# Batch 0 and batch 1 loaded and staged differently at the start of a pooled-attention and MLP kernel

## The chip, the core and the metric

The kernel runs on one core of a Trainium2 chip. A core has a matrix engine (TensorE, PE in the profile, with its weight loads as PEld), VectorE (DVE), ScalarE (ACT), GpSimd (POOL) and SyncE (SP), and 16 DMA engines that serve the queues of SP, ACT and POOL. In the traces q1 is SP's queue, q10 ScalarE's and q0 GpSimd's, whose transfers also convert fp32 to bf16. The metric is the device time of one execution in microseconds. Four executions of the kernel before took 300.72 to 301.33, median 301.1.

## The reference

q, k and v have 8 batches, 8 heads, 576 tokens and 64 elements a head. k and v are averaged over 8 neighbouring tokens to 72 rows; each batch then does softmax attention. The result, 4608 tokens of 512, goes through a two-layer MLP whose activation is h - tanh(h).

```python
k_p = k.reshape(B, H, Sp, pool, D).mean(axis=3)
v_p = v.reshape(B, H, Sp, pool, D).mean(axis=3)
scores = scale * np.matmul(q, k_p.transpose(0, 1, 3, 2))
attn = softmax(scores)
x = np.matmul(attn, v_p).transpose(0, 2, 1, 3).reshape(B * S, H * D)
h = x @ w_in
out = (h - np.tanh(h)) @ w_out
```

## The kernel before

Attention goes batch by batch, the MLP in 9 groups of 512 tokens. A group has a hidden stage (`mlp_h`: 16 tiles of 4 matmuls, tanh on ScalarE, the difference `gT` on VectorE) and an output stage (`mlp_o`: 4 token blocks of 16 matmuls, in 16 units u of 4 matmuls). The attention of batch g+1 stands between the units of group g's output stage. The order on every engine is the order in which the code is written (`manual_schedule`).

Two heads share 144 pooled rows of k (or v), laid on partitions: the first 128 rows of each of four head pairs form the main tiles 0 to 3, the remaining 16 of each pair form tile 4, the leftovers (`NM`). `pool_k` adds the eight tokens in three steps and writes each row twice (`kd`), TensorE turns it (`turn_tile`), and `kb_main` and `kb_left` place it in `KB`. In batch 0 v is pooled by TensorE instead (`v_pe_pool`, accumulating 8 matmuls against `ident`, or against `spread` for the leftovers); in the others `pool_v` does it with adds. `av_half` multiplies the exponentials `E` with `VB`, divides by the sum that an extra column carries, and writes `x_sb`; `x_pe_transpose` turns that into `xT`, from which `mlp_h` reads.

q has 512 tokens in four interleaved columns (R = 4) and a tail of 64 tokens (`QT`, `load_q_tail`), which come as separate loads, are cast to bf16 (`q_cast`, or `q_turn` for batch 0) and turned by TensorE for batches 0 and 1 (`q_pe_transpose`, `q_pe_tail`), by DMA for the others.

At the start SP loads k of batch 0, ScalarE's queue loads q and the leftovers, and GpSimd's queue loads v of batch 0 (L576), the four quarters of w1 (L503) and the first two of w2 (L510). k of batch 1 waits for the second quarter of w1 (L592, `after`), then come q and v of batch 1 on SP. ScalarE also issues q's tail of batch 0 (L640), v's leftovers of batch 1 (L659, four DMAs) and q's tail of batch 1 (L660). While the data come, `warm_pe` puts matmuls on zeros into TensorE's gaps, 29 in all.

Batch 0's attention (L631 to L690) goes through eight `av_half` and eight `x_pe_transpose` of two feature blocks each; five hidden tiles of group 0 are begun early with two of their four matmuls. Batch 0's last 64 tokens, which belong to group 1, are done in group 0's hidden stage: the tail's turn after tile 7, its scores after 9, its attention after 11, its turn into xT after 13. GpSimd pools k of batch 1 at L707, with the last two quarters of w2 issued between its first and second step. In group 0's output stage batch 1 is done: q cast at u=0, k turned at u=2, q turned at u=3 to 5, v pooled at u=4 (VectorE), scores at u=4 to 8, attention of its five blocks from u=9, each turned two units later.

In the built program a DMA of SP or ScalarE carries one of eight semaphores in turn, so each waits for the DMA eight places before it to land. PSUM has eight banks: three for hidden tiles, two for outputs, three for attention (`ps_a`); within group 0's output stage attention has only the last three (`ps_b1`).

```python
for u in range(16):
    qd, tb = u // 4, u % 4
    mlp_o(0, tb, qd * 4, qd * 4 + 4, gts, o_pools[tb])
```

Of the kernel before, what the change touches and what calls it, by code (L numbers as in the profile page):

```python
# [8 lines left out]
FP32 = mybir.dt.float32  # L9
# [10 lines left out]
R = 4  # L20
QA = 128 * R
QT = S - QA
T = B * S
# [14 lines left out]
def kernel(  # L38
# [19 lines left out]
    ps_h = ctx.enter_context(tc.tile_pool(name="ps_h", bufs=3, space=PSUM))  # L58
    ps_o = ctx.enter_context(tc.tile_pool(name="ps_o", bufs=2, space=PSUM))
    ps_a = ctx.enter_context(tc.tile_pool(name="ps_a", bufs=3, space=PSUM))  # L60
# [9 lines left out]

    w1b = const.tile([128, NFB, DFF], BF16, name="w1b")
# [3 lines left out]
    spread = const.tile([128, 128], BF16, name="spread")  # L75
    mask = const.tile([128, 3 * NM, 1], FP32, name="mask")
# [3 lines left out]
    q_bf = const.tile([128, R + 1, H, D], BF16, name="q_bf")  # L80
    warm = const.tile([128, 1], FP32, name="warm")
# [22 lines left out]
    def load_left(src, dst, b, eng=nc.sync):  # L104
        return [
            eng.dma_start(out=dst[32 * t : 32 * t + LO, NM, :], in_=src[b, 128:PR, t, :])
            for t in range(NM)
        ]
# [5 lines left out]

    def load_k(b):
        return [
            load_main(k_pairs, k_raw[b % 2], b, 0, NM),
            load_dense(k_pairs, k_raw[b % 2], b),
        ]

    def load_v(b):
        return [load_main(v_pairs, v_raw[b % 2], b, 0, NM)] + load_left(
            v_pairs, v_raw[b % 2], b
        )

    def load_q_tail(b, t, eng):
        eng.dma_start(
            out=t[:QT, :, R, :], in_=q[b, :, QA:S, :].rearrange("h p d -> p h d")
        )

    def load_q(b, tail=True):
        if b not in q_raws:
            q_raws[b] = raw.tile([128, H, R + 1, D], FP32, name="q_raw", tag="q_raw")
        t = q_raws[b]
        nc.sync.dma_start(
            out=t[:, :, 0:R, :], in_=q[b, :, 0:QA, :].rearrange("h (p j) d -> p h j d", j=R)
        )
        if tail:
            load_q_tail(b, t, nc.sync)
# [4 lines left out]
    def q_cast(b, eng=nc.gpsimd.tensor_copy, parts=1):  # L144
        t = q_raws.pop(b)
        n = H // parts
        for h in range(0, H, n):
            eng(  # L148
                out=q_bf[:, 0:R, h : h + n, :].rearrange("p j h d -> p h j d"),
                in_=t[:, h : h + n, 0:R, :],  # L150
            )
        eng(out=q_bf[:QT, R, :, :], in_=t[:QT, :, R, :])

    def q_dma_transpose(b):
        qT = work.tile([128, NHP, S], BF16, name="qT", tag="qT")
        for j in range(R + 1):
            rows = 128 if j < R else QT
            nc.sync.dma_start_transpose(
                out=qT[:, :, j * 128 : j * 128 + rows],
                in_=q_bf[:rows, j, :, :].rearrange("p h d -> p (h d)"),  # L160
            )
        qTs[b] = qT

    def q_pe_transpose(b, hps, eng=None):
        if b not in qTs:
            qTs[b] = work.tile([128, NHP, S], BF16, name="qT", tag="qT")
        qT = qTs[b]
        for hp in hps:
            ps = ps_any([128, QA], FP32, "qT_ps")
            for j in range(R):  # L170
                nc.tensor.matmul(  # L171
                    ps[:, j * 128 : (j + 1) * 128],
                    lhsT=q_bf[:, j, 2 * hp : 2 * hp + 2, :].rearrange("p h d -> p (h d)"),
                    rhs=ident[:, :],
                    start=True,
                    stop=True,
                )
            evac(qT[:, hp, 0:QA], ps[:, :], eng)

    def q_pe_tail(b):  # L180
# [9 lines left out]
        evac(qTs[b][:, :, QA:S], ps[:, :, :])  # L190
# [23 lines left out]
    def pool_v(b, eng):  # L214
# [10 lines left out]
        v_main(VB[b % 2], r[:, :, 0:1, :], eng, 0, NM)  # L225
        v_left(VB[b % 2], r[:, NM, 0:1, :], eng)

    def v_main(vb, vs, eng, t0, t1):
# [3 lines left out]
            in0=vs[:, t0:t1, :, :].to_broadcast([128, n, 2, D]),  # L232
# [4 lines left out]
        )  # L237

# [27 lines left out]

    def k_transpose(b, alloc, engs=(nc.vector.tensor_copy, nc.scalar.copy)):
# [5 lines left out]
        ps = alloc([128, 128], FP32, "kT_ps")  # L273
        turn_tile(ps[:, :], kd, NM)
# [18 lines left out]
    def score_mms(b, t, dst, c0, c1, pairs=range(NM)):  # L293
        for m in pairs if t == NM else (t,):
# [11 lines left out]
    def scores(b, t):  # L306
        if t == 0:
            E_tiles[b] = work.tile([128, NT, S], BF16, name="E", tag="E")
        E = E_tiles[b]
        hs = S // 2  # L310
        pss = []
        for half in range(2):
            ps = ps_a.tile([128, hs], FP32, name="s_ps", tag="ps_a")
            score_mms(b, t, ps[:, :], half * hs, (half + 1) * hs)
            pss.append(ps)
        for half, ps in enumerate(pss):
            nc.scalar.activation(  # L317
                out=E[:, t, half * hs : (half + 1) * hs], in_=ps[:, :], func=ACT.Exp, scale=SCALE
            )
# [377 lines left out]
    for i in range(5, NHID):  # L697
        mlp_h(0, i, gts)
        if i == 7:
            q_pe_tail(0)  # L700
# [104 lines left out]
```

The softmax here doesn't subtract the row's maximum and nothing guards it: scores larger than these inputs give would overflow.

## Time and profile before

| what | value |
|---|---|
| median of 4 runs | 301.1 us (300.72 to 301.33) |
| the profiled execution | 300.72 us, its span 299.0 us |
| TensorE busy | 291.5 us, 98% of the span |
| VectorE, ScalarE, GpSimd busy | 159.2, 149.4, 115.2 us |
| MLP matmuls, hidden and output | 126.9 and 134.4 us busy |
| granted TensorE clock | 1.00 throughout |
| DMA, first 60 us | 15.53 MB, mean 259 GB/s |

A span is the time from the first to the last instruction of the profiled execution. Busy times of TensorE are taken instruction by instruction, and matmuls overlap: a 128x512 matmul is given with 0.38 us, while one starts every 0.216 us in an unbroken row. So the time that work takes on TensorE is read from the distance of starts, not from the busy time of one. A "<-" in brackets behind a line names what the engine had waited for, and for how long.

The loads of the start land as follows (issue, time to landing, in us): v of batch 0 3.67 + 8.5; w1's quarters 5.1 + 10.3, 5.85 + 12.8, 6.6 + 15.4, 7.3 + 19.0; w2's first two 8.04 + 23.2 and 11.24 + 24.4, the others 32.98 + 8.7 and 33.7 + 9.6; k of batch 1 18.66 + 10.7, its q 19.87 + 16.6, its v 29.40 + 11.2.

### The profile page before, as it was taken

To read this page: it belongs to the slowest core of one execution; us is meant where nothing else is said; L and a number is where in the kernel's file an instruction comes from. 1 tells how busy PE (TensorE), PEld (TensorE's weight loads), DVE (VectorE), ACT (ScalarE), POOL (GpSimd) and SP (SyncE) were. 2 spreads that over 40 slices of the span, in tenths; PEclk is the share of its full clock that TensorE was granted. 3 is DMA by queue.
4 is the path that set the end of the run, shared out by engine and by line. 5 is a ranking of instruction groups with operands and counts; after the bars stand their busy time and mean duration, and the time that the engine had idled before them with its cause. 6 is when DMAs were issued, how large, how long until landed. Compare 5 with 4: busy or idle time off the path is not lost.

```text
span 299.0 us, 4694 instructions
## 1 busy us (share of the span) xinstructions
PE 291.5 (98%) x1671; PEld 142.4 (48%) x1671; DVE 159.2 (53%) x343; ACT 149.4 (50%) x283; POOL 115.2 (39%) x110
## 2 busy tenths in 40 slices
PE   7989999999999999999999999999999999999994
PEld 3444455544544454445544554455445544444443
DVE  5658665673547444753476247716680758108600
ACT  4647683666146623654265516650665166126511
POOL 8500905870495109924961079408930000000000
PEclk9999999999999999999999999999999999999999
DMA  7999999849854997798648974796421430111032
GB/s 258 221 210 280 312 223 315 259 100 331 217 114 101 280 296 128 120 322 217 108 87 242 309 156 88 261 293 148 96 59 35 91 97 0 37 70 36 2 70 70
DMA packets 66183, 49.79 MB, mean 167 GB/s; under 512 B 39920, under 2 KB 52976, under 8 KB 66160
## 3 DMA queue, kind: packets, MB, share of 16 engines
q1 hardware_dynamic: 58832, 42.94, 55.1%
q0 software_dynamic: 4752, 4.72, 9.4%
q10 hardware_dynamic: 2576, 1.84, 2.2%
q8 instruction: 13, 0.21, 0.3%
q14 instruction: 10, 0.08, 0.1%
HBM read 36.70 MB, written 9.44 MB: 154 GB/s over the span
## 4 chain that ended last, share of the span: by engine, by line
PE 85%; DMA 9%; POOL 4%; issue 0%; SPq 0%; ACT 0%; DVE 0%; POOLq 0%
PE o_ps L456 40%; PE hT_ps L428 37%; DMA w1b<-in_moe_w_in_dram 4%; PE x_ps L346 4%; DMA k_raw<-in_k_dram 4%; PE s_ps L298 3%; POOL k_raw L198 1%; DMA out_dram<-o_sb 1%; POOL k_raw L203 1%; POOL kd L206 1%; POOL w2b L510 0%; PE xT_ps L390 0%; POOL v_raw L576 0%; PE qT_ps L171 0%; POOL w1b L503 0%
## 5 line engine op out<-in xcount | busy, mean ns | idle before, releaser
L456 PE MATMUL o_ps<-w2b,gT 128*128 128x512 bf16 x560 | 134.4, 380 | 0.0
L441 DVE TENSOR_TENSOR gT<-hT_ps,t_sb 128x512 bf16<-128x512 f32 x144 | 98.9, 691 | 57.7 <-ACT t_sb L439 57.6
L428 PE MATMUL hT_ps<-xT,w1b 128*128 128x512 bf16 x576 | 126.9, 379 | 0.3 <-ACT xT L397 0.3
L439 ACT ACTIVATE t_sb<-hT_ps 128x512 f32<-128x512 f32 x144 | 85.6, 597 | 38.3 <-PE hT_ps L428 37.5
L428 PEld LDWEIGHTS <-w1b 128*128 128x128 bf16 x576 | 55.9, 98 | 66.5 <-issue 0.4
L456 PEld LDWEIGHTS <-gT 128*128 128x128 bf16 x560 | 52.5, 98 | 52.1 <-issue 1.4
L465 ACT COPY o_sb<-o_ps 128x512 f32<-128x512 f32 x33 | 19.3, 585 | 75.2 <-PE o_ps L456 75.2
L359 DVE RECIPROCAL rden<-x_ps 128x4 f32<-128x4 f32 x80 | 14.2, 177 | 52.8 <-PE x_ps L346 52.3
L360 DVE TENSOR_TENSOR x_sb<-x_ps,rden 128x256 bf16<-128x256 f32 x80 | 34.0, 425 | 3.6 <-DMA xT<-x_sb 0.7
L148 POOL CAST q_bf<-q_raw 128x2048 bf16<-128x2048 f32 x6 | 11.3, 1888 | 59.8 <-DMA out_dram<-o_sb 36.1
L198 POOL TENSOR_TENSOR k_raw<-k_raw 128x1280 f32<-128x1280 f32 x7 | 20.2, 2887 | 27.1 <-DMA k_raw<-in_k_dram 27.1
L317 ACT ACTIVATE E<-s_ps 128x288 bf16<-128x288 f32 x60 | 21.4, 410 | 13.2 <-PE s_ps L298 13.0
L346 PE MATMUL x_ps<-VB,E 128*128 128x130 bf16 x240 | 20.8, 221 | 0.7 <-ACT xT L397 0.6
L346 PEld LDWEIGHTS <-E 128*128 128x128 bf16 x240 | 16.9, 98 | 9.2 <-issue 0.8
L216 POOL TENSOR_TENSOR v_raw<-v_raw 128x1280 f32<-128x1280 f32 x6 | 17.4, 2898 | 0.0
L298 PE MATMUL s_ps<-qT,KB 128*128 128x288 bf16 (+5 forms) x128 | 17.0, 290 | 0.1
L298 PEld LDWEIGHTS <-KB 128*128 128x128 bf16 (+1 forms) x128 | 7.0, 96 | 10.1 <-issue 3.4
L527 PE MATMUL warm_ps<-xT 128*128 128x512 bf16 x29 | 10.1, 461 | 1.3 <-DVE xT L539 1.3
L206 POOL TENSOR_TENSOR kd<-k_raw 128x640 bf16<-128x640 f32 x7 | 10.8, 1538 | 0.6
L203 POOL TENSOR_TENSOR k_raw<-k_raw 128x640 f32<-128x640 f32 x7 | 10.8, 1539 | 0.5
L397 ACT CAST xT<-xT_ps 128x256 bf16<-128x256 f32 (+1 forms) x14 | 5.8, 436 | 8.9 <-PE xT_ps L390 8.7
L219 POOL TENSOR_TENSOR v_raw<-v_raw 128x640 f32<-128x640 f32 x6 | 9.3, 1545 | 0.5
(73 smaller groups left out, 100.6 us busy)
## 6 DMA issues: line engine op xcount, KB each, us to landing
k_raw<-in_k_dram SPq DMA_DIRECT2D x7, 1024.0 KB, 6.0
q_raw<-in_q_dram SPq DMA_DIRECT2D x7, 1024.0 KB, 9.7
v_raw<-in_v_dram SPq DMA_DIRECT2D x7, 1024.0 KB, 9.0
out_dram<-o_sb SPq DMA_DIRECT2D x38, 128.0 KB, 2.4
out_dram<-o_sb SPq DMA_DIRECT2D x16, 256.0 KB, 3.0
w1b<-in_moe_w_in_dram POOLq DMA_DIRECT2D x4, 512.0 KB, 14.1
w2b<-in_moe_w_out_dram POOLq DMA_DIRECT2D x4, 512.0 KB, 16.9
k_raw<-in_k_dram SPq DMA_DIRECT2D x7, 128.0 KB, 5.9
```

What stands on the lines that cost most here:

```text
L198: first = eng.tensor_tensor(out=r[:, :, 0:4, :], in0=r[:, :, 0:4, :], in1=r[:, :, 4:8, :], op=ALU.add)
L216: eng.tensor_tensor(out=r[:, :, 0:4, :], in0=r[:, :, 0:4, :], in1=r[:, :, 4:8, :], op=ALU.add)
L298: nc.tensor.matmul(dst[p : p + w], lhsT=KB[b % 2][:, o : o + w], rhs=qTs[b][:, m, c0:c1], start=True, stop=True,)
L317: nc.scalar.activation(out=E[:, t, half * hs : (half + 1) * hs], in_=ps[:, :], func=ACT.Exp, scale=SCALE)
L346: nc.tensor.matmul(ps[:, 2 * n : 2 * n + 2, :].rearrange("p h d -> p (h d)") if n < 2 else ps.rearrange("p (a s) d -> p a s d", s=2)[:, :, ...
L359: nc.vector.reciprocal(out=rden[:, :, :], in_=ps[:, :, D:D1])
L360: nc.vector.tensor_tensor(out=x_sb[:, half, :, :], in0=ps[:, :, 0:D], in1=rden[:, :, :].to_broadcast([128, 4, D]), op=ALU.mult,)
L428: nc.tensor.matmul(h_tiles[i][:, :], lhsT=w1b[:, fb, i * 128 : (i + 1) * 128], rhs=xT[:, fb, tok0 : tok0 + TG], start=(fb == 0), stop=(fb ...
L439: nc.scalar.activation(out=t_sb[:, :], in_=h_ps[:, :], func=ACT.Tanh)
L441: nc.vector.tensor_sub(out=gT[:, :], in0=h_ps[:, :], in1=t_sb[:, :])
L456: nc.tensor.matmul(o_ps[:, :], lhsT=gts[i][:, tb * 128 : (tb + 1) * 128], rhs=w2b[:, i, :], start=(i == 0), stop=(i == NHID - 1),)
L465: (nc.vector.tensor_copy if g == 0 and tb % 2 else nc.scalar.copy)(out=o_sb[:, :], in_=o_ps[:, :])
```

## The change

- The leftovers of batches 0 and 1 come as half rows (4 of the 8 tokens) over all 128 partitions, as `load_halves`, in place of whole rows over 64 partitions or, for v of batch 1, of four DMAs. The two halves of a row are joined by the matmul that turns them: k's leftovers are added in two VectorE (batch 0) or GpSimd (batch 1) steps into an fp32 tile `k_left` and turned against the fp32 `twos`; v's of batch 0 are pooled with four matmuls against a `spread` that has two ones a column, and v's of batch 1 are added into the fp32 `vl` and spread by one fp32 matmul.
- The loads of batch 1 on SP are in the order k, halves of k, halves of v, q's tail of batch 0, q in two DMAs, v. ScalarE issues no DMA after its first five. q of batch 1 has nine neighbouring tokens a partition (`q_nine`, 2304-byte rows), so that it has no separate tail; its output rows are stored in the matching order (`NINE`, `out_segments`).
- w2's second quarter, and those after it, wait for k of batch 1; the third and fourth are issued between GpSimd's steps on k.
- v of batch 0 is pooled in two halves. The attention of batch 0 is divided in pairs of blocks, two PSUM banks with one reciprocal and one multiply (`av_pair`), and turned in pairs (`x0_turn`). PSUM is one tile with banks named by hand. 24 warm-up matmuls are left of 29.
- Batch 0's last 64 tokens move from group 0's hidden stage to its output stage (u=0, 1, 8, 11). Batch 1's steps there stand one unit later, each unit is cut in two for the last turn at u=15, and batch 1's last block moves to group 1's hidden stage.
- Later loads of k (from batch 3 on) and v (from batch 6 on) are cut in two DMAs.

```diff
+    def load_halves(src, dst, b, eng=nc.sync):
+        return eng.dma_start(out=dst[:, NM, 0:HALF], in_=src[b, 2 * 128 : 2 * PR, :, :])
+    q_nine = q.rearrange("b (s a h) (p j) d -> b s p a h (j d)", s=2, a=2, j=NJ)
...
+    def pool_k_left(b, eng):
+        r = k_raw[b][:, NM, 0:HALF].rearrange("p (j d) -> p j d", d=D)
+        eng.tensor_tensor(out=r[:, 0:2, :], in0=r[:, 0:2, :], in1=r[:, 2:4, :], op=ALU.add)
+        eng.tensor_tensor(
+            out=k_left[b][:, :, :],
+            in0=r[:, 0:1, :].to_broadcast([128, 2, D]),
+            in1=r[:, 1:2, :].to_broadcast([128, 2, D]),
+            op=ALU.add,
+        )
+    def pool_v1(eng):
...
+        eng.tensor_tensor(out=vl[:, :], in0=r[:, NM, 0, :], in1=r[:, NM, 1, :], op=ALU.add)
...
+    def v1_left():
+        ps = ps_any([128, 1, D], FP32, "v_ps")
+        nc.tensor.matmul(ps[:, 0, :], lhsT=spread32[:, :], rhs=vl[:, :], start=True, stop=True)
+        v_left(VB[1], ps, nc.vector)
+    def turn_left(dst, b):
+        nc.tensor.matmul(
+            dst, lhsT=k_left[b].rearrange("p a d -> p (a d)"), rhs=twos[:, :], start=True, stop=True
+        )
...
-    nc.vector.memset(k_raw[0][:, NM, :], 0.0)
-    nc.vector.memset(v_raw[1][:, NM, :], 0.0)
...
+    nc.gpsimd.memset(q_bf[64:128, R, :, :], 0.0)
+    nc.gpsimd.memset(spread[:, :], 0.0)
     nc.gpsimd.dma_start(out=v_bf[:, 0:NM, :], in_=v_pairs[0, 0:128, :, :])
-    nc.gpsimd.memset(spread[:, :], 0.0)
+    nc.gpsimd.tensor_tensor(out=twos.rearrange("p (x t) -> p x t", t=NM), ...)
...
-    load_w2(1)
-    after(load_k(1), w1_dmas[1])
-    load_q(1, False)
+    k1 = load_main(k_pairs, k_raw[1], 1, 0, NM)
+    after([k1], w1_dmas[1])
+    load_halves(k_halves, k_raw[1], 1)
+    load_halves(v_halves, v_raw[1], 1)
+    load_q_tail(0)
+    load_q_nine(1, 0, nc.sync)
+    load_q_nine(1, 1, nc.sync)
     load_main(v_pairs, v_raw[1], 1, 0, NM)
+    load_w2(1)
+    after(w2_dmas[1:], k1)
+    pool_k(1, nc.gpsimd, 0, NM)
+    load_w2(2)
+    pool_k_left(1, nc.gpsimd)
+    load_w2(3)
...
+    def av_pair(p, half, b0):
+        ps = PS[:, b0 : b0 + 2, 0 : 4 * D1].rearrange("p k (h d) -> p k h d", d=D1)
+        for k in range(2):
+            av_mms(0, 2 * p + k, half, ps[:, k, :, :])
+        rden = work.tile([128, 2, 4, 1], FP32, name="rden2", tag="rden2")
+        nc.vector.reciprocal(out=rden[:, :, :, :], in_=ps[:, :, :, D:D1])
+        nc.vector.tensor_tensor(out=x0[:, 2 * p : 2 * p + 2, half, :, :], in0=ps[:, :, :, 0:D], ...)
...
+    av_pair(0, 0, 2)
+    av_pair(1, 0, 5)
+    av_pair(0, 1, 0)
+    warm_pe(1)
+    x0_turn((0, 1), 0, 7, nc.scalar.copy)
+    av_pair(1, 1, 2)
+    warm_pe(1)
+    x0_turn((2, 3), 0, 5, nc.scalar.copy)
+    warm_pe(2)
+    h_open(3, 4)
+    x0_turn((0, 1), 1, 7, nc.scalar.copy)
+    h_open(0, 0)
+    h_open(1, 1)
+    x0_turn((2,), 1, 5, nc.scalar.copy)
+    x0_turn((3,), 1, 6, nc.vector.tensor_copy)
+    h_open(2, 2)
+    h_open(4, 3)
...
-        if i == 7:
-            q_pe_tail(0)
-        if i == 9:
-            scores_tail(0)
-        if i == 11:
-            x4 = av(0, 4, ps_any, False)
-        if i == 13:
-            x_pe_transpose(0, 4, x4)
...
-        mlp_o(0, tb, qd * 4, qd * 4 + 4, gts, o_pools[tb])
+        mlp_o(0, tb, qd * 4, qd * 4 + 2, gts, o_pools[tb])
+        if u == 15:
+            x_pe_transpose(1, *pend.pop(0))
+        mlp_o(0, tb, qd * 4 + 2, qd * 4 + 4, gts, o_pools[tb])
+        if u == 0:
+            q_four_tail(0)
+        if u == 1:
+            scores_tail(0)
+        if u == 8:
+            x4 = av(0, 4, ps_any, False)
+        if u == 11:
+            x_pe_transpose(0, 4, x4)
+        if u == 1:
+            q_nine_cast(1, nc.scalar.copy, 0, 2, 0, 4)
+            q_nine_cast(1, nc.scalar.copy, 0, 2, 4, NJ)
+        if u == 3:
             k_transpose(1, ps_any, (nc.vector.tensor_copy, nc.vector.tensor_copy))
+        if u == 4:
+            q_pe_transpose(1, 0, 0, "act")
+            q_pe_transpose(1, 0, 4, "act")
+        if u == 5:
+            q_pe_transpose(1, 1, 0, "act")
+            pool_v1(nc.vector)
+        if u == 6:
+            q_pe_transpose(1, 1, 4, "act")
+        if 5 <= u <= 9:
+            scores_wide(1, (u - 5,))
+        if u == 9:
+            v1_left()
+        if u == 10:
+            q_pe_tail(1)
+        if u == 11:
+            scores_tail(1)
+        if u >= 10:
+            if 12 <= u < 15:
                 x_pe_transpose(1, *pend.pop(0))
             if u <= 13:
+                pend.append((u - 10, av(1, u - 10, ps_any, False)))
...
+            if g == 1 and i == 0:
+                x4 = av(1, 4, ps_b1, False)
+            if g == 1 and i == 3:
+                x_pe_transpose(1, 4, x4)
```

## The prediction

> **What bounds the kernel now.** I read the windows first, then TensorE's timeline up to the second group, ScalarE's beside it, the chain of waits and the DMA queues. The windows cut the span where the stages change: start, hidden matmuls of group 0, its output matmuls with batch 1's attention between them, and the rest. Columns: stretch, length, busy time of TensorE, its weight loads, VectorE, ScalarE and GpSimd, granted clock, DMA share, GB/s.
>
> ```profile
> 0.00:20.68 20.68, 17.49 (x121) 8.69 (x122) 13.61 (x43) 10.68 (x21) 10.51 (x27) 1.00 1.06 233
> 20.68:34.82 14.14, 13.83 (x83) 6.54 (x81) 10.32 (x20) 10.44 (x20) 4.67 (x4) 1.00 1.15 266
> 34.82:54.90 20.08, 19.92 (x157) 10.96 (x156) 12.33 (x32) 12.05 (x21) 8.74 (x5) 1.00 1.05 291
> 54.90:299.00 244.10, 240.29 (x1318) 116.21 (x1315) 122.95 (x250) 116.19 (x221) 91.31 (x75) 1.00 0.58 145
> ```
>
> From 20.68 on TensorE is full, and the last 244 us stay as they are. So only two things can move the end: how early TensorE gets dense work, and whether data then keep up, for the DMA share is above 1 up to 54.9. In the start, ScalarE is held by its own DMA issues: L127 waits until 16.55 us for an older load, so the first xT copy, whose matmuls stood at 15.63, runs at 17.22, and TensorE waits for it at 17.64.
>
> ```profile
> 13.16 1.76 ACTq L106 DMA_DIRECT2D v_raw<-in_v_dram  x4
> 16.55 0.62 ACTq L127 DMA_DIRECT2D q_raw<-in_q_dram  x1
> 17.22 0.65 ACT L397 CAST xT<-xT_ps 128x256 bf16<-128x256 f32 x2 [3.53 <-PE xT_ps L390]
> ```
> ```profile
> 14.54 0.69 PE L346 MATMUL x_ps<-VB,E 128*128 128x130 bf16 x9
> ...
> 17.64 0.34 PE L346 MATMUL x_ps<-VB,E 128*128 128x130 bf16 x3 [0.63 <-ACT xT L397]
> ...
> 20.68 5.78 PE L428 MATMUL hT_ps<-xT,w1b 128*128 128x512 bf16 x26
> ```
>
> The chain of waits (start, length, what) shows the other limit: w1's second quarter lands at 18.66, k of batch 1 starts only then, and its pooled tile reaches TensorE at 37.74, with no slack. v of batch 1 lands at 40.64, where VectorE waits for it.
>
> ```profile
> 5.85 12.79 DMA w1b<-in_moe_w_in_dram
> 18.66 0.37 SPq L102
> 19.13 10.84 DMA k_raw<-in_k_dram
> ...
> 37.74 0.45 PE kT_ps L259 x5
> ```
> ```profile
> 40.64 1.49 DVE L216 TENSOR_TENSOR v_raw<-v_raw 128x1280 f32<-128x1280 f32 x1 [1.40 <-DMA v_raw<-in_v_dram]
> ```
>
> **Start.** ScalarE loses its six late DMA issues, so its 3.5 us gap goes. k's leftover is two VectorE adds of 128x128 (0.29 each, L206's row) for three (0.42+0.58+0.29). The first v lands at 3.67+8.5=12.2; pooled in two halves (8 matmuls at 0.056=0.45, then 0.42 on VectorE) it lets the first attention matmul go at 13.2, for 14.54. Eight reciprocal-and-multiply steps (0.17+0.42) become four over 128x512. No row shows that form; its multiply lies between 0.69 (gT, same size) and twice 0.42; I take 0.69, so 0.85 a pair, and VectorE ends at 17.2 for 20.32. The second pair's copy (0.6) ends at 16.6; from there ten hidden matmuls (0.216 each, 2.16) and eight transposes (0.45) run on, to 19.2. Before, 20.68 stood with six such matmuls done. Ahead: 1.5 + 4 x 0.216 = 2.3 us. It is 0.9 if w1's second quarter or the first v holds it, 3.0 if all pairs cost 0.6. Five of 29 warm-up matmuls go; they fill gaps only. VectorE's two memsets (0.48 each) lay in a wait for k.
>
> GpSimd's new small steps (three memsets, two copies, an add, some 0.25 to 0.3 each) lie mostly after 10.7, in its idle 16.6 us before k. Some 0.25 us stands ahead of v's issue and 0.5 ahead of w1's; the software queue moved no packet before 8 us, so both are hidden; without that cover they cost just that.
>
> **First hidden stage.** The last 64 tokens of batch 0 leave it: 4+8+6+4 small matmuls, 0.12+0.25+0.35+0.12=0.84. Its 58 matmuls take 12.5 of 14.14; 0.84 is moved and 0.8 is loss around the moved work (0.31 shown at 33.03). Group 0's output stage then starts at 34.82-2.3-0.84-0.8=30.9. w2's first quarter landed at 8.04+23.2=31.3, and earlier after the change (below), so I count 0 here, 0.4 if not.
>
> **Output stage of group 0.** Work: 20.08-0.16 of wait, +0.84 taken in, -0.47 (batch 1's last block goes to group 1), +0.3 for three fp32 matmuls: 20.6. A fp32 128x64 matmul is in no row: between 0.04 (bf16, 8 in 0.32) and 0.216 (512 columns); 0.1 each is nearer the former. The page "FP8 and Floating Point Precision" of the Trainium skill (TensorE Precision Notes) says that true fp32 takes four passes; by that the three cost 0.5, and the sum rises by 0.2.
>
> The deadlines move up with TensorE:
> - k: SP's queue holds k, the halves, q's tail, q in two parts, v. ScalarE's queue had moved 0.13 MB between 12 and 16 us, mostly 256-byte packets; the software queue then made 165 GB/s, and 182 between 18.6 and 22 with half as much beside it. Without it w1's second quarter lands some 0.6 earlier and k at 27.9 for 29.4. GpSimd then issues w2 (0.75), pools four tiles (2.35+1.28+1.28, on the slope of L198 and L203), issues w2 (0.75) and adds the leftover (2 x 0.47): 35.4. TensorE wants it at 35.0: 0.4 of stall.
> - q: 35.2, after that ScalarE's two casts (1.04+1.28) end at 37.5, wanted at 36.4: 1.1, the 0.4 within it.
> - w2's second quarter, now issued after k: about 35, wanted at 35.3.
> - v decides. VectorE runs its instructions in order: the pooling of v (u=5) stands ahead of the division of batch 0's last block (u=8), whose results hold two of three PSUM banks; the fifth score tile (u=9) takes the first of them again. So TensorE stops at u=9 until v has landed, been pooled (1.23+0.86+0.25+0.45+0.73=3.5) and two divisions are done (1.2). With the spread matmul: v's landing + 4.9. From there to group 1: six units of 0.863, and 0.12+0.25+4 x 0.35+0.12+4 x 0.22 of attention, 7.9 to 8.0; then 0.55 because the last xT copy starts half a unit before it is read, behind two other copies on ScalarE (0.58 each). Group 1 starts at landing + 13.4.
>
> When does v land? 40.64 before. Earlier by 1.0: 1.76 MB of software traffic after 8.2 us at 187 for 168 GB/s. Earlier by 1.2: q in 2304-byte rows for 1 KB and 256 bytes (the 1 KB rows moved at 127 GB/s on 45% share, the 2 KB rows at 157 on 46%). Later by 1.3: 128 KB of v's halves and q's 256-byte tail now stand ahead of it. I take 39.7. Bounds: 38.5 if w2's last quarters fall behind it, 42.0 if nothing is won and the additions count.
>
> A rule speaks against this: "DMA: Bandwidth & Descriptors" of the Trainium skill (Issuing engines are not separate DMA queues) says that moving loads between issuing engines changes only issue time. By that v stays at 40.64 and the gain is nil, 301.1.
>
> **Sum.** Group 1 starts at 39.7+13.4=53.1 for 54.9; its hidden stage takes in 0.47 and, as VectorE has 1.2 of division between its 0.69 steps, some 0.4 of stall: 0.9 gained, span 298.1. The profiled run took 300.72 around 299.0, 0.4 under the median of 301.1. Against the median: 300.2.
>
> **Rivals.**
> - v comes early and gates nothing. For it: the issue of v no longer waits for k (29.40 before). Against: the order in the queue is the same, and q is behind. TensorE's own work gives 30.9+20.6+0.55=52.05, with 0.4 of stall and the 0.87: 1.6 gained, 299.5; with the larger start 298.8.
> - v lands as before: the time is unchanged, 300.6 to 301.7. For it: above all the share of 1.05 to 1.15; bytes are only moved about. Against: q's longer rows.
> - The slower side: batch 1's v lands at 41.2 or later and blocks VectorE, and through the bank TensorE at u=9. It decides from 41.2 on; at 42.0 group 1 starts at 55.4, plus 0.87: 1.4 lost, 302.5. For it: 0.26 MB more in the SP queue ahead of v than before. Against: the time won ahead of 18 us.
> - The clock falls as warm-up matmuls go: granted 1.00 with 1.37 of 2 us busy around 17 us; not counted.
>
> **Numbers.** Forecast 0.37 (299.6 to 300.6), early v 0.20, unchanged 0.20, slower 0.23. Some 0.2% (0.6 us) is what can be told from no change here: faster 0.57, same 0.20, slower 0.23. Range 298.8 to 302.0; the likeliest case alone 299.6 to 300.6.
>
> **What would show it.** Right: no ScalarE DMA issue after 4 us, first attention matmul near 13.2, dense hidden matmuls by 19.2, output stage from about 31, a TensorE wait for VectorE at the fifth score tile, group 1 near 53. Wrong: waits of the output matmuls for w2, or a wait at the k leftover over 1 us; then the queue order, not v, sets the time. A start no earlier than 20 us would take the base away, and a wait in group 2 for batch 2's loads would add a loss that I have put at nothing (2.7 us of slack: KB done at 67.74, read at 70.43).

## The result and the profile after

The changed kernel takes 301.37 us in the median of 53 runs, the kernel before 300.96 in 79 runs beside it. The ratio of the means is 1.0023, 95% interval 1.0013 to 1.0032: 0.23% slower on average, where the forecast was 0.9 us faster. The 53 runs fall into two groups by TensorE's granted clock: 38 with a mean clock of 0.997 or more (below: full clock) took 300.77 to 301.94, median 301.13, and 15 with 0.994 took 302.57 to 303.86, median 303.03. The mean of the first group is only 0.05% above that of the kernel before, which cannot be told from no change, so most of the 0.23% is the lower clock of the second group. The profiled execution belongs to the first; it has a span of 299.6 us, for 299.0 before.

The windows of the changed kernel, cut where the stages change (the hidden stage of group 1 is a row of its own here; columns as in the prediction):

```profile
0.00:19.13 19.13, 16.28 (x121) 8.45 (x122) 11.16 (x32) 10.56 (x18) 10.44 (x30) 1.00 1.03 233
19.13:31.89 12.76, 12.68 (x62) 5.66 (x59) 9.58 (x16) 9.02 (x17) 4.15 (x3) 1.00 1.14 284
31.89:55.12 23.23, 20.85 (x170) 11.89 (x169) 12.48 (x33) 13.17 (x24) 9.83 (x9) 1.00 1.09 278
55.12:69.66 14.54, 14.43 (x74) 6.78 (x74) 10.85 (x20) 9.22 (x16) 10.29 (x10) 1.00 0.59 160
69.66:299.60 229.94, 226.48 (x1253) 110.04 (x1251) 112.47 (x235) 106.85 (x205) 81.14 (x65) 1.00 0.58 143
```

Set against the same stages before, the lengths say where the time went. The forecast column is worked out from the prediction's own times; its start is counted with six hidden matmuls begun, as both traces have it.

| stage, us | before | after | forecast |
|---|---|---|---|
| start, to the dense hidden matmuls | 20.68 | 19.13 | 18.4 |
| hidden stage of group 0 | 14.14 | 12.76 | 12.5 |
| output stage of group 0 | 20.08 | 23.23 | 22.2 |
| hidden stage of group 1 | 13.80 | 14.54 | 14.67 |
| the rest | 230.30 | 229.94 | 230.30 |

The first two stages gain 2.93 us. The output stage was to grow by 2.1, because it takes in work and waits for v; it grew by 3.15. In it TensorE is busy for 20.85 of 23.23 us, so what is lost there is a wait and not work. (The rest, where later loads of k and v are cut in two, is 0.36 us shorter; no run tells why.) TensorE's waits up to 80 us name it (what waited, for whom: us in all, times, longest):

```profile
PE PS L608 <- DMA w2b<-in_moe_w_out_dram: 2.0, 1, 2.0
...
PE PS L580 <- ACT xT L550: 0.3, 1, 0.3
```

Before the change no output matmul waited for w2. The chain of waits of the changed kernel (start, length, what) runs through that load:

```profile
17.49 9.87 DMA k_raw<-in_k_dram
27.36 0.29 issue
27.65 10.79 DMA w2b<-in_moe_w_out_dram
38.44 0.04 issue
38.48 1.02 PE PS L608 x4
```

k of batch 1 lands at 27.36, 2.04 us sooner than before. Only then GpSimd issues w2's second quarter, which needs 10.79 us. The first output matmul that reads it stands ready at 36.44 and starts at 38.48.

The start went in the forecast direction. TensorE's timeline:

```profile
13.86 1.21 PE L507 MATMUL PS<-VB,E 128*128 128x130 bf16 x18
...
17.39 0.59 PE L580 MATMUL PS<-xT,w1b 128*128 128x512 bf16 x2 [0.24 <-ACT xT L846]
...
18.04 1.03 PE L580 MATMUL PS<-xT,w1b 128*128 128x512 bf16 x4
...
19.13 1.24 PE L580 MATMUL PS<-xT,w1b 128*128 128x512 bf16 x5
```

The first product with v stands at 13.86 (14.54 before, 13.2 forecast), and dense hidden matmuls follow 5.27 us later (6.14 before). But only six hidden matmuls are begun ahead of 19.13, not ten.

### The profile page after: what moved, and what is told of

It is laid out like the page before. It is cut to its first block, busy times and chain, and to the rows that moved or that the text cites. A ratio compares the mean times of both kernels' runs of the same rounds, so it can differ in the third digit from the quotient of the medians.

```text
span 299.6 us, 4716 instructions
## 1 busy us (share of the span) xinstructions
PE 290.7 (97%) x1672; PEld 142.8 (48%) x1672; DVE 156.6 (52%) x333; ACT 148.8 (50%) x279; POOL 115.9 (39%) x116
## 4 chain that ended last, share of the span: by engine, by line
PE 83%; DMA 11%; POOL 2%; DVE 1%; ACT 1%; issue 1%; SPq 0%; POOLq 0%; ACTq 0%
PE PS L608 39%; PE PS L580 36%; PE PS L507 4%; DMA w1b<-in_moe_w_in_dram 4%; DMA w2b<-in_moe_w_out_dram 4%; DMA k_raw<-in_k_dram 3%; PE PS L451 3%; DMA out_dram<-o_sb 1%; DVE gT L593 0%; ACT xT L550 0%; POOL v_raw L722 0%; PE PS L264 0%; DVE x_sb L493 0%; ACT o_sb L617 0%; POOL w1b L663 0%
## 5 line engine op out<-in xcount | busy, mean ns | idle before, releaser
L608 PE MATMUL PS<-w2b,gT 128*128 128x512 bf16 x560 | 134.6, 380 | 2.0 <-DMA w2b<-in_moe_w_out_dram 2.0
L593 DVE TENSOR_TENSOR gT<-PS,t_sb 128x512 bf16<-128x512 f32 x144 | 98.9, 691 | 57.2 <-ACT t_sb L591 57.2
L580 PE MATMUL PS<-xT,w1b 128*128 128x512 bf16 x576 | 126.6, 379 | 0.8 <-ACT xT L550 0.3
L591 ACT ACTIVATE t_sb<-PS 128x512 f32<-128x512 f32 x144 | 85.6, 597 | 39.1 <-PE PS L580 38.9
L580 PEld LDWEIGHTS <-w1b 128*128 128x128 bf16 x576 | 56.2, 98 | 68.4 <-issue 1.7
L617 ACT COPY o_sb<-PS 128x512 f32<-128x512 f32 x33 | 19.3, 585 | 75.5 <-PE PS L608 75.5
L493 DVE TENSOR_TENSOR x_sb<-PS,rden 128x256 bf16<-128x256 f32 x72 | 30.6, 425 | 2.7 <-DMA xT<-x_sb 0.2
L469 ACT ACTIVATE E<-PS 128x288 bf16<-128x288 f32 x60 | 21.4, 410 | 13.2 <-PE PS L451 13.0
L301 POOL TENSOR_TENSOR k_raw<-k_raw 128x1280 f32<-128x1280 f32 (+1 forms) x7 | 19.7, 2809 | 12.1 <-DMA k_raw<-in_k_dram 12.1
L507 PE MATMUL PS<-VB,E 128*128 128x130 bf16 x240 | 20.2, 221 | 0.1
L451 PE MATMUL PS<-qT,KB 128*128 128x288 bf16 (+5 forms) x128 | 17.1, 289 | 0.1
L451 PEld LDWEIGHTS <-KB 128*128 128x128 bf16 (+1 forms) x128 | 7.1, 96 | 9.6 <-issue 3.0
L309 POOL TENSOR_TENSOR kd<-k_raw 128x640 bf16<-128x640 f32 (+1 forms) x7 | 10.5, 1504 | 0.5
L306 POOL TENSOR_TENSOR k_raw<-k_raw 128x640 f32<-128x640 f32 (+1 forms) x7 | 10.5, 1497 | 0.5
```

The source lines that it names most:

```text
L301: first = eng.tensor_tensor(out=r[:, :, 0:4, :], in0=r[:, :, 0:4, :], in1=r[:, :, 4:8, :], op=ALU.add)
L451: nc.tensor.matmul(dst[p : p + w], lhsT=KB[b % 2][:, o : o + w], rhs=qTs[b][:, m, c0:c1], start=True, stop=True,)
L469: nc.scalar.activation(out=E[:, t, c0:c1], in_=ps, func=ACT.Exp, scale=SCALE)
L493: nc.vector.tensor_tensor(out=x_sb[:, half, :, :], in0=ps[:, :, 0:D], in1=rden[:, :, :].to_broadcast([128, 4, D]), op=ALU.mult,)
L507: nc.tensor.matmul(ps[:, 2 * n : 2 * n + 2, :].rearrange("p h d -> p (h d)") if n < 2 else ps.rearrange("p (a s) d -> p a s d", s=2)[:, :, ...
L580: nc.tensor.matmul(h_tiles[i][:, :], lhsT=w1b[:, fb, i * 128 : (i + 1) * 128], rhs=xT[:, fb, tok0 : tok0 + TG], start=(fb == 0), stop=(fb ...
```

## The experiments

A w2 quarter is called by its place; the second is the one that moved. The expectations call experiments 1 to 9 e1 to e9. Times are medians; ratios are of means, to the kernel before in the same series, with 95% intervals.

**1. The quarter issued where it was before** (after GpSimd's cast of v's leftovers, waiting for nothing).

```diff
     nc.gpsimd.tensor_copy(out=v_bf[:, NM, 0:HALF], in_=v_raw[1][:, NM, 0:HALF])
+    load_w2(1)
...
-    load_w2(1)
-    after(w2_dmas[1:], k1)
     pool_k(1, nc.gpsimd, 0, NM)
     load_w2(2)
+    after(w2_dmas[2:], k1)
```

> The changed kernel with one edit: w2's second quarter is issued where the kernel before issues it (behind the cast of v's leftover, with no wait for k of batch 1). Theory A (the wait of 2.04 us for that quarter at u=4 is what the change lost): the wait goes, v of batch 1 (VectorE starts on it at 39.7) then stops TensorE at u=9 for some 0.4 to 1.0, and the time falls by 1.0 to 1.6 us against the changed kernel, some 0.3 to 0.9 under the kernel before. Rival B (the DMA engines are full, so what comes earlier makes something else later): k or q of batch 1 lands 1 to 2 us later, TensorE waits for them instead at u=3 or u=4, and the time stays within 0.4 us of the changed kernel. Rival C (the loss sits in the moved blocks and the fp32 matmuls): the wait goes and TensorE is still behind at group 1.

Measured: 300.16 us, ratio 0.9971 (0.9957 to 0.9984). This one edit turns a loss of 0.23% into a gain of 0.29%. All eleven runs had full clock, so against the changed kernel's runs at full clock it is 300.16 for 301.13 us. The wait for w2 is gone. TensorE's waits between 30 and 60 us:

```profile
PE PS L230 <- ACT q_bf L207: 0.6, 1, 0.6
PE PS L580 <- ACT xT L550: 0.3, 1, 0.3
```

0.63 us came in for it: ScalarE's cast of batch 0's q tail is late, as w2 now shares the DMA engines when that tail is loaded (it landed at 33.0, in the changed kernel at 30.8).

**2. The wait taken away, the loads left as they are.** Tiles 4 to 7 of group 0's output stage read the first quarter of w2 in place of the second, so the output is not the reference's.

```diff
-                rhs=w2b[:, i, :],
+                rhs=w2b[:, i - 4 if g == 0 and 4 <= i < 8 else i, :],
```

> The changed kernel, but in group 0 the output matmuls of hidden tiles 4 to 7 read w2's first quarter in place of the second; all loads stay as they are, so only the wait is taken away, and that part of the sums is other than the reference's. Theory A: TensorE has no wait at u=4, u=9 waits for v's pooling until about 44.6 (0.4 to 0.6 us), and the time is 1.3 to 1.7 us under the changed kernel. Rival B gives the same here, since the traffic is unchanged; rival C: less than 0.8 us.

Measured: 299.52 us, ratio 0.9945 (0.9926 to 0.9964), 1.61 us under the changed kernel's runs at full clock (301.13). The output stage takes 21.64 us for 23.23, 1.59 less. So 1.6 of the 2.04 us reaches the end. The rest came back: TensorE waits 0.32 us for w2's third quarter, and 0.14 ahead of the matmul that spreads v's leftovers. Group 1 starts at 53.14; the forecast for a kernel without this wait was 53.1.

**3. The kernel before, with ScalarE's six late DMA issues on SP behind k.**

```diff
-    nc.scalar.dma_start(out=t0[:QT, :, R, :], in_=q[0, :, QA:S, :].rearrange("h p d -> p h d"))
...
-    load_left(v_pairs, v_raw[1], 1, nc.scalar)
-    load_q_tail(1, q_raws[1], nc.scalar)
...
+    load_q_tail(0, t0, nc.sync)
     load_q(1, False)
+    load_q_tail(1, q_raws[1], nc.sync)
+    load_left(v_pairs, v_raw[1], 1)
```

> The kernel before, with ScalarE's six late DMA issues (q's tail of batch 0, v's leftovers and q's tail of batch 1) moved to SP's queue behind k of batch 1. Theory A (ScalarE's wait for a DMA slot holds the start): the first xT copy runs at about 16.0 for 17.22, TensorE's 0.6 us wait at 17.6 goes, dense hidden matmuls start 0.6 to 1.0 us earlier; k lands 0.5 to 1 earlier too. Whether the end follows depends on q, which stands behind one more 256-byte load: 0 to 0.8 us faster. Rival: the start is set by VectorE's divisions, and the gain is under 0.3 at 20.68.

Measured: 316.77 us, ratio 1.0474 (1.0427 to 1.0521), where at most the time of the kernel before was expected. The chain of waits shows why:

```profile
18.43 12.67 DMA q_raw<-in_q_dram
31.10 0.02 issue
31.12 0.62 ACT q_bf L691
31.74 0.50 ACT t_sb L439
32.24 0.02 issue
32.26 0.70 DVE gT L441
32.97 0.04 issue
33.01 4.09 PE hT_ps L428 x12
```

In this kernel ScalarE casts the q tail ahead of the tanhs of group 0's first tiles. The tail, now behind k, landed at 31.1, and the tanhs stood behind the cast. TensorE waited 9.9 us, and its clock fell with it: 0.74 granted from 20 to 40 us. The start, where the clock was 1.00, can still be read from TensorE's timeline, and there the theory held: dense hidden matmuls begin at 19.92 for 20.68. From the first product with v at 14.46 it takes 5.46 us, for 6.14 before.

**4. The kernel before, with the second quarter issued only after k.**

```diff
     nc.gpsimd.tensor_copy(out=v_bf[:, NM, :], in_=v_raw[1][:, NM, :])
-    load_w2(1)
...
-    after(load_k(1), w1_dmas[1])
+    k1 = load_k(1)
+    after(k1, w1_dmas[1])
+    load_w2(1)
+    after(w2_dmas[1:2], k1[0])
```

> The kernel before, with one part of the change alone: w2's second quarter is issued only when k of batch 1 has landed. Theory A (a quarter takes some 9 to 11 us from issue to landing while SP's queue is full): k lands at about 28.5, the quarter at 38 to 39.5, the output matmuls of u=4 (39.4) wait 0 to 0.5 us, and the time is within 0.4 us of before; so the same wait costs little here, because TensorE comes 3 us later. Rival D (from issue to landing it takes the 4 to 5 us that a quarter takes in the row of quarters): it lands by 34, and nothing waits.

Measured: 318.68 us, ratio 1.0569 (1.0524 to 1.0614). It tells nothing of w2. ScalarE's timeline shows a hold in another place:

```profile
28.41 0.62 ACTq L127 DMA_DIRECT2D q_raw<-in_q_dram  x1
29.07 0.92 ACT L397 CAST xT<-xT_ps 128x256 bf16<-128x256 f32 x3 [15.40 <-DMA k_raw<-in_k_dram]
```

The edit changed which of the eight DMA semaphores each load gets. The q tail of batch 1, issued from ScalarE, got that of k and could not be issued before k had landed; xT's copies stood behind it, and TensorE waited 12.5 us for them. The loss of some 18 us is larger than that wait, as the granted clock was 0.66 from 20 to 40 us.

**5. The second quarter with SP's queue kept free**: SP holds q (and v behind it) until the quarter has landed.

```diff
-    load_q_nine(1, 0, nc.sync)
+    load_w2(1)
+    after(w2_dmas[1:], k1)
+    q1 = load_q_nine(1, 0, nc.sync)
+    after([q1], w2_dmas[1])
     load_q_nine(1, 1, nc.sync)
...
-    load_w2(1)
-    after(w2_dmas[1:], k1)
```

> The changed kernel with the loads of batch 1's q (both halves) and of v behind them held on SyncE until w2's second quarter has landed. In the changed kernel that quarter was issued at 27.65, moved 0.13 MB up to 33.0 and landed at 38.44. Theory (it stood behind what SyncE had already queued: k's and v's leftovers, q, v): with q and v out of the way it moves at some 200 GB/s from about 29 and lands by 33.5. Rival (a load of the software queue takes this long from its issue whatever else is queued; the later quarters took 8.0 and 8.9 us): it lands at 35.6 to 38.4. Either way q comes late and the kernel is slower: q lands some 7 us after w2, so TensorE waits at the sixteenth to twentieth matmul group of the output stage, 304 to 308 us in all.

Measured: 309.44 us in one run, above the expected 304 to 308; TensorE waits 8.3 us for q's casts, and its mean clock is 0.983. The chain of waits has the quarter's transfer, and q's behind it:

```profile
27.23 5.98 DMA w2b<-in_moe_w_out_dram
...
33.88 9.64 DMA q_raw<-in_q_dram
```

It lands at 33.21, 5.98 us after its issue for 10.79. The rival (a fixed time from issue) is refuted. What each queue moved between 28 and 32 us (packets, MB, share of the 16 engines), first in the changed kernel, then here, then in experiment 1:

```profile
q1 hardware_dynamic: 963, 1.29, 106.4%
q0 software_dynamic: 16, 0.01, 2.0%
```
```profile
q0 software_dynamic: 488, 0.49, 85.8%
q1 hardware_dynamic: 384, 0.11, 11.5%
```
```profile
q0 software_dynamic: 500, 0.49, 72.6%
q1 hardware_dynamic: 730, 0.46, 46.3%
```

In all three the quarter had been issued before 28. In the changed kernel the first quarter was all but through, and the software queue moved 0.01 MB in 4 us while SP took all engines; the second quarter's packets began at 32.1, 4.5 us after its issue. With SP's queue run down they began at 28.7, 1.5 us after the issue, and the queue moved 0.49 MB. In experiment 1 the quarter had been queued since 11.35, and the queue also moved 0.49 MB with SP at work.

**6. Experiment 1 with two loads back on ScalarE's queue**, where the kernel before has them.

```diff
-    load_halves(v_halves, v_raw[1], 1)
-    load_q_tail(0)
...
     scores_wide(0, (0, 1))
+    load_q_tail(0, nc.scalar)
...
     v_main(VB[0], v_b, nc.vector, 2, 4)
+    load_halves(v_halves, v_raw[1], 1, nc.scalar)
```

> e1 (w2's second quarter issued early) with two loads put back on ScalarE's queue where the kernel before has them: batch 0's q tail after the second wide score and the leftovers of batch 1's v after batch 0's pooled v. Theory (part of the start's gain is ScalarE's time on issuing; the kernel before with these issues moved off showed 0.76 us): the first dense hidden matmul is 0.5 to 0.8 us later than e1's 19.31, and as TensorE has only small waits behind it, the total is 0.3 to 0.8 us above e1's 300.16 (q's tail then lands early, which gives back up to 0.6 us of e1's wait for its cast). Rival (the start's gain is all from the joined divisions and turns): start within 0.2 of e1's, total 299.5 to 300.2.

Measured: 314.06 us, ratio 1.0429 (1.0402 to 1.0456). Missed by 13 us, and neither theory was tested. In the profiled execution, which took 330.73 us, the leftovers' issue went out only at 28.03, with xT's copies behind it, and TensorE waited 12.1 us for them. The profile names no releaser for it; GpSimd starts on k, which it had waited for, at 28.04, so the issue most likely waited for k's semaphore, as in experiment 4.

**7. Experiment 1 with batch 0's q tail ahead of the leftovers on SP.**

```diff
+    load_q_tail(0)
     load_halves(k_halves, k_raw[1], 1)
     load_halves(v_halves, v_raw[1], 1)
-    load_q_tail(0)
```

> e1 with batch 0's q tail issued ahead of k's and v's leftovers on SyncE. In e1 its cast was late and TensorE waited 0.63 us for it at the first output tile. Theory: that wait goes, k's leftovers land some 1 us later (TensorE waited nothing for them in the output stage) and the kernel takes 299.5 to 299.8, the fastest so far but for the one that reads another quarter of w2. Rival (the wait comes back at k's leftovers or at q's casts, as the same bytes are queued): 300.0 to 300.3.

Measured: 299.97 us, ratio 0.9976 (0.9959 to 0.9994), between the two expectations. The 0.63 us wait for the tail's cast is gone; 0.2 us came back at q's casts. The difference to experiment 1 lies inside the intervals.

**8. The second quarter released by w1's last quarter**, at 24.57 instead of 27.65. (The later quarters stand behind GpSimd's steps on k in any case.)

```diff
-    after(w2_dmas[1:], k1)
+    after(w2_dmas[1:2], w1_dmas[3])
```

> The changed kernel with w2's second quarter held only until w1's last quarter has landed (about 25.0), not until k has (27.4). Theory (a load that enters while SyncE's queue is full stands behind what is queued): it still moves little before 30, lands at 34 to 36.5, in time or nearly, and the kernel takes 299.6 to 300.4. Rival (only the time of issue counts, 10.8 us to landing as before): it lands at 36.0 and TensorE waits at most 0.2 us, 299.4 to 299.8; and if w2 was not the cause at all the kernel stays at 301.2 to 301.5.

Measured: 300.20 us, ratio 0.9983 (0.9973 to 0.9992). The quarter landed 11.1 us after its issue, at 35.7, ahead of its use, and the wait is gone; 0.26 us came back at q's casts. So 3.1 us of issue time turn the loss into a gain. The first quarter was still moving when the second was issued (0.32 MB of the software queue up to 27.5), and yet that queue moved only 0.02 MB from 27.5 to 29.5. The second quarter's packets began 4.9 us after their issue, much as in the changed kernel (4.5), experiment 9 (25.63 to 30.2, 4.6) and the kernel before (third quarter, 32.98 to 37.0, 4.0). Beside a full SP queue the moment of issue counted, then, and not whether the software queue was empty; experiment 5 shows that the delay is no fixed time.

**9. A version that gathers what was learned**: experiments 7 and 8, and batch 1's last block multiplied with v ahead of group 1's first hidden tile, to fill the wait for xT there.

```diff
             mlp_h(g, i, gts)
             if g == 1 and i == 0:
                 x4 = av(1, 4, ps_b1, False)
...
+            if g == 1 and i == 0:
+                x4 = av(1, 4, ps_b1, False)
+            mlp_h(g, i, gts)
```

> The changed kernel with w2's second quarter released by w1's last (as in e8_w2_mid), batch 0's q tail issued ahead of the leftovers (as in e7_tail_first), and batch 1's last block multiplied with v ahead of group 1's first hidden tile instead of behind it. Theory: the 0.34 us that TensorE waits at the boundary for xT's copy is filled with these 0.35 us of matmuls; 0.2 to 0.5 us below e8's 300.20 and e7's 299.97, so 299.5 to 299.8. Rival (something behind gives it back: VectorE's divisions come ahead of the first hidden tile's subtraction): the wait moves to the second or third hidden tile and the total stays at 299.9 to 300.3.

Measured: 299.56 us, ratio 0.9947 (0.993 to 0.9963). It is faster than both kernels. TensorE's waits from 30 to 60 us:

```profile
PE PS L608 <- DMA w2b<-in_moe_w_out_dram: 0.4, 1, 0.4
PE PS L451 <- DVE x_sb L493: 0.3, 1, 0.3
PE PS L360 <- DVE x_sb L493: 0.2, 1, 0.2
```

The boundary wait of 0.34 us (L580 in the lists above) is gone. The quarter, issued at 25.63 in this execution, landed at 36.7 and was 0.4 us late again. v landed at 40.55, and here the fifth score tile (L451) and the matmul that spreads v's leftovers (L360) wait for VectorE's divisions, as the prediction had it.

**10. That version with batch 0's last block ahead of v's pooling on VectorE.**

```diff
-        if u == 8:
+        if u == 4:
             x4 = av(0, 4, ps_any, False)
-        if u == 11:
+        if u == 8:
             x_pe_transpose(0, 4, x4)
```

> e9_fill with batch 0's last block moved from the ninth to the fifth group of output matmuls (its turn from the twelfth to the ninth), so that its divisions on VectorE stand ahead of v's pooling and not between the pooling and the rest. If v's landing decides the output stage, as the prediction had it, the divisions behind the pooling are part of that chain, and the stage ends 0.5 to 1.2 us sooner. If TensorE's own work decides and v has slack, the stage changes by less than 0.25 us (only the small gap ahead of the fifth score tile goes), and the total is within 0.3 us of e9_fill's.

Measured: 299.52 us, ratio 0.9953 (0.9934 to 0.9971), the same as experiment 9. The output stage took 21.98 us for 22.39, between the two expectations. The waits of L451 and L360 are gone, and one of 0.8 us came at q's turns, which need the bank that the early block still holds:

```profile
PE PS L264 <- DVE x_sb L493: 0.8, 1, 0.8
```

No gain of 0.5 us or more appeared, but with this new wait the run does not decide how much slack v has.

**11. Experiment 8 with the q tail's issue alone back on ScalarE.**

```diff
-    load_q_tail(0)
...
     scores_wide(0, (0, 1))
+    load_q_tail(0, nc.scalar)
```

> e8_w2_mid with the issue of batch 0's q tail put back on ScalarE's queue behind the second wide score, where the kernel before has it. Theory (its 0.64 us of issuing on ScalarE stands in the chain of casts, turns and exponentials): the first product with v comes 0.4 to 0.7 us later than the 13.47 to 14.21 of the runs with the issue on SyncE, the 5.27 us from there to the dense hidden matmuls stay, and the total is 300.4 to 300.9 against e8's 300.20. Rival (the chain on VectorE from k's last landing decides the start): first product with v at 13.5 to 14.2, total as e8 or 0.2 less because the tail lands early.

Measured: 301.92 us, ratio 1.0025 (1.0005 to 1.0044), 0.42 points above experiment 8. Here too the clock divides the runs: four with 0.998 or more took 300.61 to 300.85, as expected and some 0.5 us over experiment 8's 300.20, and six with 0.992 to 0.994 took 301.89 to 302.84. So at full clock one DMA issue on ScalarE costs some 0.5 us. The timeline of a run at full clock shows that the issue itself is the smaller part of what holds ScalarE:

```profile
10.51 0.64 ACTq L188 DMA_DIRECT2D q_raw<-in_q_dram  x1
11.20 1.14 ACT L201 CAST q_bf<-q_raw 128x512 bf16<-128x512 f32 x2 [2.15 <-DMA v_raw<-in_v_dram]
```

ScalarE was free from 9.05, but the load shares a semaphore with v's leftovers of batch 0, which landed at 10.5, so 1.46 of its 2.15 us of idle time were a wait for them. TensorE waited 2.1 us for the cast behind it. The first product with v came at 15.43 instead of 13.47 to 14.21, more than the 0.4 to 0.7 expected. The time from there to the dense matmuls stayed at 5.26 us.

**12. Experiment 8 with batch 0's divisions done singly.**

```diff
+        for k in range(2):
+            rden = work.tile([128, 4, 1], FP32, name="rden", tag="rden", bufs=4)
+            nc.vector.reciprocal(out=rden[:, :, :], in_=ps[:, k, :, D:D1])
+            nc.vector.tensor_tensor(out=x0[:, 2 * p + k, half, :, :], in0=ps[:, k, :, 0:D], ...)
...
```

> e8_w2_mid with the joined divisions of batch 0's start done singly: per pair two reciprocals of 0.18 and two products of 0.42 us for one of 0.20 and one of 0.69, 0.31 us more on VectorE for each of four pairs. In six profiles of kernels with joined divisions the time from the first product with v to the dense hidden matmuls was 5.27 us; in the kernel before 6.14. Theory (the joining earns these 0.87 us): 5.27 becomes 5.9 to 6.5, total 0.6 to 1.2 us over e8's 300.20. Rival (ScalarE's issues, no longer in this stretch, earned it): it stays within 0.2 us of 5.27.

Measured: 300.25 us, ratio 0.9979 (0.9965 to 0.9993), as experiment 8. From the first product with v (14.03) to the dense matmuls (19.53) it takes 5.50 us for 5.27: joining the divisions earns 0.23 us. That is near the rival's 0.2 and far from the theory's 0.6 to 1.2. The rest of the 0.87 us fits ScalarE's issues, since experiment 3, with single divisions and no issues there, has 5.46.

## Why the prediction was wrong

**The step that failed** is "w2's second quarter, now issued after k: about 35, wanted at 35.3". It landed at 38.44 and was wanted at 36.44. Its wait of 2.04 us is more than the whole forecast gain, and experiments 1, 2 and 8 each remove it in another way and make the kernel faster than before (0.9971, 0.9945, 0.9983). At full clock the changed kernel took 301.13 us for the forecast 300.2; with the wait taken away alone (experiment 2) it took 299.52. The prediction shows no working for the 35, which is 7.1 us behind its k; 10.79 was measured from the issue. The rows before the change held a better price: the third and fourth quarters, issued beside the same full queue, took 8.7 and 9.6 us. From the forecast landing of k at 27.9 they give 36.6 to 37.5 against the wanted 35.3, a wait of 1.3 to 2.2 us. That 2.04 lies in it is partly luck, as the load landed later than this and TensorE also came 1.1 us later. The prediction named "waits of the output matmuls for w2" as a sign of failure, but gave that case no price, no chance and no rival. The slower rival was v; the slower result came by w2.

**The clock.** The prediction named a falling clock as a rival and did not count it. In the profiles of experiments 3 to 5 the granted clock fell from 1.00 to 0.50 when TensorE had run nothing for 2.3 to 3.1 us. In experiment 4 its last matmul ended at 16.99, the clock fell at 20.0, matmuls began again at 29.5 and the clock came back at 33.7, 4.2 us later. A mean of 0.994 over 300 us is 1.8 us lost, an estimate (0.006 x 300), and the medians of the two groups of runs lie 1.9 us apart; some 3.6 us at half clock would do it. Runs with such a clock are common in the two kernels whose longest TensorE wait is just over 2 us: 15 of 53 with w2's wait of 2.04, 6 of 10 in experiment 11 with its wait of 2.1. In the seven kernels of experiments 1, 2, 7 to 10 and 12, whose longest wait is 1.3 us, they are 1 of 57. That fits w2's wait as the cause of the second group too, but no profile was taken in such a run, so it is not shown.

**The start** was mis-sized: 1.55 us for 2.3. 5.27 us from the first product with v to dense matmuls is 0.73 us better than forecast from its own start (13.2 to 19.2, 6.0), but for six matmuls begun instead of ten, which is 0.86 less. The first product came at 13.86 for 13.2; in nine profiles with this start it stood at 13.47 to 14.21, so part of that is scatter between executions. That ScalarE's gap of 3.5 us goes was right: its first copy of xT ran at 15.91 for 17.22. Where the gain comes from was half right. The joined divisions, priced at 0.85 us a pair, are 0.20 + 0.69 as taken, but are worth 0.23 us in all (experiment 12). ScalarE's freed queue is worth more (experiments 3 and 11).

**The first hidden stage** took 12.76 us for 12.5, and the moved 0.84 and the lost 0.8 left it as said. That w2's first quarter costs nothing was right.

**k and q.** k landed at 27.36 (27.9 forecast) and made no wait in the output stage for the forecast 0.4; q's casts ended at 36.73 (37.5 forecast). The forecast waits of 1.1 us were not seen, as w2 came later than both; with w2's wait away, TensorE waited 0.26 us for q's casts in experiment 8 and not at all in experiment 2.

**v** landed at 39.7 as forecast. VectorE's timeline:

```profile
39.73 1.23 DVE L344 TENSOR_TENSOR v_raw<-v_raw 128x1024 f32<-128x1024 f32 x1 [2.42 <-DMA v_raw<-in_v_dram]
```

"v decides" did not come true in the changed kernel: from landing to group 1 it took 15.4 us and not 13.4, because w2 had already stopped TensorE. With the w2 wait away the step holds in number: 39.53 to 53.14 in experiment 2 is 13.6, 39.67 to 53.42 in experiment 8 is 13.75. The mechanism (divisions behind the pooling hold up the fifth score tile and the matmul that spreads v's leftovers) stopped TensorE for 0.26 and 0.15 us in experiment 9 and for 0.14 in experiment 2; in experiment 8 it did not. The price of this chain was right: output matmuls go on 4.96 us after v's landing in experiment 9 and 4.95 in experiment 2, for the forecast 4.9. But in experiments 2, 8 and 9 TensorE came to this point late by a wait of its own (0.32, 0.26 and 0.41 us). TensorE's own work and v's chain end within half a microsecond of each other, and the runs do not say which of the two would set the time of a kernel without other waits.

**The boundary and the fp32 matmuls.** The wait for the last xT copy was 0.34 of the forecast 0.55. A fp32 128x64 matmul costs more than the 0.1 us taken. TensorE's timeline:

```profile
46.19 0.44 PE L360 MATMUL PS<-vl,spread 128*128 128x64 f32 x2
46.47 1.03 PE L608 MATMUL PS<-w2b,gT 128*128 128x512 bf16 x4
...
55.12 1.02 PE L580 MATMUL PS<-xT,w1b 128*128 128x512 bf16 x4 [0.34 <-ACT xT L550]
```

The profile counts two instructions for one, and the next matmul starts 0.28 us later (0.24 for the one at 11.52): some eight times the 0.03 us of a bf16 matmul of this shape. The page "FP8 and Floating Point Precision" of the Trainium skill (TensorE Precision Notes) says four passes; three such matmuls, some 0.75 us, lie above the 0.5 worked out from it and well above my 0.3. My sum was wrong in the count as well: one of the three, at 11.52, stands in the start, so the output stage took in two, some 0.5 us.

**The rule weighed against the change**, that issuing engines are not queues of their own ("DMA: Bandwidth & Descriptors" of the Trainium skill, Issuing engines are not separate DMA queues), held in part. By it v would have landed at 40.64, but it landed at 39.73, with larger rows for q as well as other queues, so the run does not split the two. It speaks of issue time alone, and that is where ScalarE's gain lay, except that the issue includes the wait for a semaphore (experiment 11: 0.64 us of issue behind 1.46 of wait).

## What to carry to other kernels

A load that is moved behind another is priced by the issue-to-landing rows of its own queue under the same traffic; then its landing is held against the first instruction that reads it, and a landing as close as 0.3 us gets a case of its own. A load that enters beside a full queue is released early enough: here its packets began 4.0 to 4.9 us after the issue, whether or not the load ahead of it was still moving. And a DMA issued from a compute engine can hold that engine for another load's landing, so an edit that reorders loads has to be read for the semaphores that they then share. Where runs of one kernel fall into two groups, the granted clock of each run is read before a difference is put down to the edit.

## What the runs showed of the hardware

- A load on the software queue waited 4.0 to 4.9 us for its first packets beside SP's full queue, in four kernels (changed kernel, kernel before, experiments 8 and 9), and 1.5 us with SP's queue run down (experiment 5). In the changed kernel it was issued at 27.65, the queue moved 0.01 MB from 28 to 32 and then 0.10 MB a microsecond beside SP's 0.20. The reverse was seen too: k, issued on SP at 17.49 while the software queue was full, moved nothing before 21. "DMA: Bandwidth & Descriptors" of the Trainium skill (Queues, rings and completion order) says that an engine takes its queues in turn, a packet at a time. In steady state the trace agrees (94 and 96 packets between 33 and 34 us); in the first microseconds after an issue there are no such turns: 16 packets against 963 from 28 to 32. Whether the new load's packets were not yet in the queue or were passed over is open.
- A wait on a shared DMA semaphore held TensorE for 12.5 and 12.1 us in two kernels that were meant to change something small (experiments 4 and, most likely, 6). In the mildest case (experiment 11) it held ScalarE for 1.46 us and cost some 0.5 us at full clock.
- From the first product with v to dense matmuls, eight executions agree within 0.01 us (5.26 or 5.27), while the moment at which that stretch begins scatters by 0.74 us between them.
- The granted clock fell to 0.50 after 2.3 to 3.1 us without a matmul (experiments 3 to 5) and was back 4.2 us after matmuls resumed in experiment 4. In 15 of 53 runs of the changed kernel its mean was 0.994, and they took 1.9 us longer in the median.
